# A clamp moved from VectorE to GpSimd, and a new order of all steps, in a gated-recurrence and MLP kernel

## The chip, the cores and the metric

The kernel runs on one core of a Trainium2 chip. A core has five engines with an instruction queue each: TensorE (PE; its weight loads are listed as PEld), VectorE (DVE), ScalarE (ACT), GpSimd (POOL) and SyncE (SP). Each works through its queue in order and waits on semaphores for the others. All transfers of this kernel are issued by SP. SBUF is the memory that the engines work in, PSUM the memory that matmuls write to, DRAM the large memory outside. The metric is the time of one execution on the device in microseconds (us), lower is better; of several runs the median counts.

## The reference

Two blocks follow each other. The first is a recurrence over 768 tokens for 4 batches and 8 heads with 48 channels. Its state is a complex 48x48 matrix per head, which is turned and damped by a gate at every token:

```python
mag = np.sqrt(a_re * a_re + a_im * a_im)
scale = np.minimum(mag, 0.999) / (mag + 1e-06)
a_re_n, a_im_n = (a_re * scale, a_im * scale)
for t in range(S):
    new_re = ar * S_re - ai * S_im
    new_im = ar * S_im + ai * S_re
    S_re, S_im = (new_re + k_t v_t^T, new_im)
    y[:, :, t] = q_t S_re
```

The second takes `y` as 3072 tokens of 384 features and applies an MLP with 2048 hidden features and a slope per feature below zero:

```python
h = x @ w_in
g = np.maximum(h, 0.0) + alpha * np.minimum(h, 0.0)
out = g @ w_out
```

The two weight matrices come as 64-bit floats, everything else as 32-bit.

## The kernel before

**Gates.** The recurrence is worked off in chunks of 128 tokens. Ahead of it, nine gate tasks turn `a_re` and `a_im` into magnitudes and phases: three for the first batch (chunk 0, chunks 1 and 2, chunks 3 to 5) and two for each other batch (three chunks each). A gate task loads its rows (L248), computes magnitude and unit phase on ScalarE and VectorE (L251 to L299), multiplies the magnitudes up a tree (L316) and sends them to DRAM as `decs` (L321), and multiplies the phases up in chains (L336, L338, helper `product`), with a carry from one task to the next. L394 to L407 make the phase of each block, and L422 and L425 apply it to all tokens. The result goes to DRAM as `phs` (L427). Small operations of these tasks run on VectorE for the first batch and on GpSimd for the others. There are two buffers for gate tasks, so a later one may load when an earlier one's `phs` has landed.

**Units.** One unit is one chunk of one batch: 24 units. It loads `q` and `k` as `KQ` (L575, L577), the phases as `PP` (L586) and the magnitudes as `T` (L593), both back from DRAM in another layout, and `v` as `V` and `VL`. VectorE multiplies `KQ` by `PP` (L648). Then come six levels of distance 1, 2, 4 to 32 tokens: TensorE makes scores in PSUM (L662), VectorE multiplies `KQ` by decays from `T` (L701), ScalarE copies `W` for the next level (L719), and the scores are masked on VectorE (L686) or ScalarE (L683). Then `k` is transposed (L736, L738), TensorE forms the chunk's `k v^T` (L747), VectorE brings the state `St` forward (L777, L780), and TensorE adds up `y` (L768, L793). At the first unit of a batch `St` is loaded (L706) and multiplied by the first `k` (L709). ScalarE copies `y` out (L807), and it goes to DRAM as `ysc` (L812).

**MLP.** The tokens of the units are taken in 14 groups of 128 or 256 tokens (1, 1, ten times 2, 1, 1 units). For each group and each of 16 blocks of 128 hidden features, three matmuls make `ps_h` (L841), ScalarE makes a negated ReLU (L848), VectorE completes the slope (L850), and a matmul adds into the output (L860). That makes 224 feature groups. `ps_h` has two buffers.

**Weights.** `w_in` and `w_out` come in 16 pieces (L487). Task `to_f32` turns a piece into 32-bit floats from its two 32-bit words: ScalarE takes the absolute value of the high word (L503), VectorE raises it to at least `F64_SMALL` (L511) and shifts it left by 3 bits (L513), ScalarE prepares the low word and the sign (L505, L507), and VectorE adds the two (L515). Two buffers `top` are used in turn.

**The order.** Nothing is scheduled at run time. Every piece of work is a Python generator that yields before each of its steps; the string `ORDER` has 4316 letters, and each letter lets one generator issue its next step. So the string sets the order of the instructions in every engine's queue, SP's included:

```python
def run(self, order):
    for c in order:
        next(self.tasks[self.LETTERS.index(c)], None)
```

`A` to `I` are the nine gate tasks, `J` loads of the units, `K` the spreading of `v` in DRAM, `L` loads of `v`, `M` the weight pieces, `N` and `O` the conversion of `w_in` and `w_out`, `P` to `Z` and `a` to `m` the 24 units, `n` the loads of `xT` for the MLP, and `o` the MLP. The string was found by a planner outside the kernel. The costs and dependences in the yields (`DVE(n // 2, ta)` and the like) were input of that planner; in the kernel they do nothing.

Of the kernel before, what the change touches and what calls it, by code (L numbers as in the profile page):

```python
# [14 lines left out]
ALU = mybir.AluOpType  # L15
# [11 lines left out]
F64_SMALL = 1.125 * 2.0 ** -15  # L27


ORDER = (  # L30
    "AAAAAAAAAAAAAAAAAAAABBJBAAMMMMKMAAAAAAANNBAAAAAAAAAAAAAAABNBMAAAJAAAAAAAAAAJJBANALBABAABANBBBOBABBAB"
    "AABAAAAKAOBNABKKMBBOBBOKBBBLLLAOABBLLLLLLABMLLBABANAAAAABOABABNAAABAKBAABNNOBBBNBBBONOMLBBBBOBOBBBBB"
    "BBNBBBBNNBOBBNBBNOOOBBBBOBCBJJPCBBBBBBOBMCCCOPBJBJCBMJNBPMBNNPPBBBJPKKKKKKKKBBBCBBCBOCKCBCBCCCCPCPCK"
    "BPCPPOPJJJLJCCPNJJPNPCDDCCCCPPCPOCONCQPCOPCQPPPQPPPQPCPPQCQOCJPJPPJPPMJJNPNNNCQCQQCCOOPPPPPCPOCPCNCP"
    "PPCPNCOPCPPCJMQQLPCCQQCDCOJPCCNNMLDCONCCCCCNCCNJKMCMnKKRCCCKORNCNCJCRLJJDCCCRCCCCQCOOOCCRRCCQCOCOOMO"
    "COOCRRooooNCNKKoCooNooOKCOCLKKMKoKKDCoooCCCCooQQQQKCooRQQCCQQNQQooQDooDDLLCNoooCDQQCQoQoooooRoooQDDQ"
    "DDRLLLLLLLLDDDoDoRQRDDDCQDQDQQQRDQRJQQQEEooooRDRoooRQNEJJJoQQNQQJJQDDLDDDDSDRDROoEoooooooESSRDSDooRo"
    "NoDERRoNRoDoSDREEooooSDLLLooEDooooRRoSLLLRDDDDRooORRDDSDDEQLLLLLLLRSRDRRNRRRRDSRDDDDODDooooDDDDEoNES"
    "oJooooOSSNJJEoJRJRRRSSTLLLLLLLLooSSoooOoJRRKDDJRoELSTnOTTToSKKoDDDoooooTLoSDDDDDDDDDoSSSSoRLToEooKoT"
    "oSoooooSSoSooooooooTETDEooSLoSSLLoETDDDEDDDooooooDSoooSSSSSSTSoSJTSoDEJJEJJEKJDoooLJLDoDLLEDEEoLoSSE"  # L40
    "SSSSSTSoooJoUoTEEEEooDDooToDooooEooooooooTnLDDooooDooooooooDEUTooooooJJLDDJooooDoooEoooooooooUTooToo"
    "oLLLLLooTDTETLooooooUTEooUoTTEoDUoooTEoEUTLooTKooEUEToJToToooUETTTTTTTETEEEETJEEEFJFETUoLoUUooooooUV"
    "TLUoFoToooTTLLUUooLoToUooVFVoUoUUUUoUUoooooFoJJUUVLLTULLLLLLoooVEEEUFUVooUUUEEEooTooEEEEEEEEEEEUUVUU"
    "UJUVUVEEFooVEooooJJJJJWVooEEEEEJUoUUUVooWUVJVoUVWKWJUoUVoEVEVWoVEEJoEEEoJWWWoJJJoVVVoWVooooVWEWVVnoL"
    "LLLLoVXLLLLooooLLLEEFLVFELEEEEFoEoVooooooVVoEoWEoVoooVoooVVVVVVVVWVEVLWWWooooooJoFFWVFWWEWXFooVVWWEV"
    "WooVLLJLJVooooooooooLLLLLVFWEWWFWWFoooooooWooooVWWoooWLLLLLWWWWWoFXXFXXWEWWoFoWFXXJFJJJJLYXFoooooooo"
    "XFXXoFFFFKJJWGoWWWXooooFooooYYWYXGWWWFoXFooYXFXoooooFoYXXXYFooYFFGFoooooooooXXooYXXooXYGooFXooFXFFXo"
    "oooXXGooXXFFFoFFLnooGoGJYoGLLLLLLLLLLLLXXXXXFFFXXFFFFXFFXJYJJJJZoGoooKooYoGooJoooooooooGGoYXZYYGYFFF"
    "FFFFFFGGJZFoZoFoooZoooGGooooXYYYYXXYZZZooYYLFLLLLLLooLLLFFoLoLLZooooXXYKKFFFFYYFFZYoooooGYYoFooFFFYF"
    "LoFGYGGGFooKoJJJKKFGGGGoYYYYYYYYYJXZooooKZoJJaKKKooLFFFooZZZLoJoZLLLooFGJLLLLXLLoLoKGFFFFoFFoooooooG"  # L50
    "GGYFYZaZaaZZooZZooooGaZZFLLFJFoooooooYYYYYYooaaFoaooooaoooJooJooZaZZZaooooZoooFZnZGGaooaoGooGGooZZZZ"
    "ZZZZaZZZGJJJHaaGJbbHooooooooooooooobGaGoZGZZaaaaaJLJJabGGHZoGZZZJJbooooooGGGooGooooaLooJboaabbHHboLL"
    "ooooaboaHbLaooaooooooHooLLLoLLooLaaLLoooGGooGGbaaGGaaGGaaooGoaJGoGGGGGGGGGGGHabbcLLHaHbGcbHHHHJJJboo"
    "ooooooooJJboooobLLGGocoobobJoooobcGGGcbbbboooHoHGbccbcKJJLLLLGoooooaocLdHaLooaobaGGbcLbLKLooGGLabbba"
    "ooooooobbGbbcHbGbbboocncoooHbGGGGGGGooocHHbodoooJJoLLoHLLoLLGGGLLLGLLHoooooLLoHooHoHoooooccKdooooooH"
    "HHHHGoooooHHooodoGLHcdoocccccobbbbbbHbdJdooGooooHoodHcHdoooooooocccddocoHHHodHHJcJJJoooJcoooccocIooo"
    "odHccccccoHccdIcoodeoHJoHoodooHHHHdodHddddHccccHJeLcLJcoooLJLLLeooooooooddooccLeLJoHHooHeHHHHHHHHedd"
    "dLIeoLooodooHHddooooLLdoLLoJJdeHHHdddddIIdddonoILJodoeoooooeLooILLfoooHHHHHHoeeooJooJIooKKoooooeHHfd"
    "dfIfodLeoeLKeKfoKKoeoodoLddIdLJJffLLLLLLeeofoeeIoofeooeooooIeooIofHHIJHHIdoIIeeooJoooHHHooeKHHoIIeoe"
    "ooeeeofHHoooeHHHHeeeeeIHLILLoooeIoeJeJJffooooooooooooKeoffgJffooooooIIoooooooooLLHHooIHHIIIfeeeeegoo"  # L60
    "ofoooeegooooooooLfffffooooooofgfggJooofLfJooLfooLLfLKHgLofLLgoofogJoffffffffIgffnooogogooJJJhIIIIooL"
    "oooIIhogoohJoooohIgLfJffLLgooooofffoIggoooooooooohLhLLLIgghgIggJLgLLgJooIooooggohgoIoIghofoooooohhgI"
    "IogoIIhgooohooooooLIIILIggggggggIJJhJooJhhgLLLhhiohoooooooIIoooohhhhhooooohohJooJgIIIIIIhhLLLIIIILhI"
    "IiooLooggooggihhhIoiooogoooooohIIIILIgJLLLLLoohoooooioIIooIIIIoIoohhohhhhhhihJoJnJiiiJJJJooooooooohI"
    "IIIIIIiooIjooIIoIIioiooIoooIIIooooojijiiooooooooLoojiooooIoojhLiILLiLLIoLoooiiiiJoLLooLooohLhooooIho"
    "ihhihjjooiooooiioiijjoooiiojiLLLioiiiioooJJJjjiiiioooLoooJjjioojjojJokooooooooojjikiiijjjJJkLoooijoo"
    "oookokkjjLkoooLookojkojkoojiijjnooookojoooooooookjLLLoLooLLLLLLjjjjjJJJkJJjJLoooooLLLLLoojjjoooooooo"
    "ooooolJJLoooollLjjjkjjojkkloooooooooooooooljjLkkkkklkLkllkJooooooooooolllkLklkJJLJLoooooolLkooookook"
    "kkooooooookkkkkkkkkJJoomooooooookkmkkkloollooooooJJokmooookknloooooooooommlmLoollmlLlloooooooloLoooo"
    "ooooooomoLllmmLLLooooooooolooooooooooollloooolloooomLoLoLLLLLllllllmlmmmoomoooooooooooooollmooooolll"  # L70
    "lllmomlmmmmmLooooooooLLoLLLoooLLLooLooooooooooooooooooooooooooooooooolnooooooomooooooooooooooooomooo"
    "ooooooooooooomoooomoomooooLooLLoomooooooooommooommmmmmmmmmmmmmmnoooooooooooooooooooooooooooooooooooo"
    "oooooooooooooooooooooooooooooooooooooooooooooooooooooooooooooooooooooooooooooooooooooooooooooooooooo"
    "oooooooooooooooo")

# [27 lines left out]
def kernel(  # L103
# [32 lines left out]
    nc = tc.nc  # L136
    B, HP, _, D, S = q.shape
    H = 2 * HP
# [60 lines left out]
    DVE = ACT = POOL = PE = DMA = step  # L199
# [290 lines left out]
    def to_f32(dst, *key):  # L490

        n = 2 * DM
        ta = yield ACT(n + 100, ("raw", *key), takes=(R["top"],))
        raw = raws.pop(key)
        lo, hi = raw[:, :, :, 0], raw[:, :, :, 1]
        slot = slots.pop(0)
        top = tops[slot].rearrange("p (r e) -> p r e", r=dst.shape[1])
        top_u = top.bitcast(U32)

        def halfwords(z, dtype=U16):  # L500
            return z.rearrange("p r e -> p (r e)").bitcast(dtype)

        nc.scalar.activation(top, hi.bitcast(F32), AF.Abs)  # L503
        tl = yield ACT(n + 200)
        nc.scalar.activation(dst, lo, AF.Identity, scale=2.0 ** -51, bias=bias_two)  # L505
        tl = yield ACT(n + 100)
        nc.scalar.activation(halfwords(dst, BF16)[:, 1::2].rearrange("p (r e) -> p r e", r=dst.shape[1]), hi.bitcast(F32), AF.Sign, bias=bias_plus)  # L507
        raw_done(*key, tl)

        yield DVE(n // 2, ta)  # L510
        nc.vector.tensor_scalar(out=top, in0=top, scalar1=F64_SMALL, scalar2=None, op0=ALU.max)  # L511
        yield DVE(n // 2)
        nc.vector.tensor_scalar(out=top_u, in0=top_u, scalar1=3, scalar2=None, op0=ALU.logical_shift_left)  # L513
        t = yield DVE(n, tl)
        nc.vector._custom_dve(ADD32_U16LIMBS, out=halfwords(dst), in0=halfwords(top), in1=halfwords(dst))  # L515
        slots.append(slot)
        return t
# [125 lines left out]
    def unit(u):  # L643
# [59 lines left out]
        if c == 0:  # L703
            k_ = yield DMA(144, *[("state", u - 2)] * (u > 1), takes=(R["St"],))
# [3 lines left out]
            k_ = yield DVE(H * D, k_, ("start", 0))  # L708
            nc.vector.tensor_tensor(out=St, in0=St, in1=start[:, b].unsqueeze(2).to_broadcast([D2, H, D]), op=ALU.mult)  # L709
            state[b] = (St, k_)  # L710
        k_ = r
        for h in LEVELS:
# [12 lines left out]
            k_ = yield DVE(2 * H * HC, e, *[("decays", u)] * (h == 1))  # L725
# [23 lines left out]
        ek = e  # L749
# [23 lines left out]
        for s in range(1 if last else 2):  # L773
            before, known = states[s]
            k_ = yield DVE(H * D, known, takes=(R["St"],))
            St = work.tile([D2, H, D], F32, tag="St", name="St", bufs=3)
            nc.vector.tensor_tensor(out=St, in0=before, in1=T[:, :, TL - 4 + s:TL - 3 + s].to_broadcast([D2, H, D]),  # L777
                                    op=ALU.mult)
            k_ = yield DVE(H * D, ek)
            nc.vector.tensor_tensor(out=St, in0=St, in1=kv[s][0:D2], op=ALU.add)  # L780
            R["lv" if s else "misc"].put(k_)
            states.append((St, k_))
# [170 lines left out]
```

## Time and profile before

| | us |
|---|---|
| median of 5 runs | 866.51 |
| lowest and highest of them | 862.18, 868.98 |
| the profiled execution | 871.17 |
| span of the profiled execution, first to last instruction | 869.5 |
| TensorE busy | 713.3 |
| VectorE busy | 650.3 |
| ScalarE busy | 428.0 |
| GpSimd busy | 164.4 |

"Busy" is the time in which an engine has at least one instruction under way. A row of a group gives the line in the kernel, the engine, the operation, what is written and read with its shape (partitions x elements), the count, the busy time, the mean duration in nanoseconds, and the idle time of the engine before these instructions with what ended it. A row of the table of waits gives who waited for whom, the total, the times and the longest. A row of the timeline gives start and duration in us. The granted clock is the share of TensorE's full clock that it was given; over the whole span it was 0.957.

### The profile page before, as it was taken

How to read it: one execution, taken by the hardware profiler on the slowest of the kernel's cores; microseconds unless marked ns; L12 is line 12 of the kernel's file. 1: busy time of each engine (PE TensorE's matmuls, PEld its weight loads, DVE VectorE, ACT ScalarE, POOL GpSimd, SP SyncE). 2: the span in 40 equal slices, each digit the busy share in tenths (PEclk: the TensorE clock that was granted, in tenths of full speed). 3: DMA queues.
4: the chain of work that ended last, by engine and by line, in shares of the span. 5: the costliest groups of instructions: out<-in, count | busy, mean ns of one | idle time of the engine just before them, and what ended most of it. 6: DMA issues, size and time to landing. Idle time of an engine off the chain costs nothing.

```text
span 869.5 us, 26876 instructions
## 1 busy us (share of the span) xinstructions
PE 713.3 (82%) x11488; PEld 532.8 (61%) x11488; DVE 650.3 (75%) x1012; ACT 428.0 (49%) x913; POOL 164.4 (19%) x277
## 2 busy tenths in 40 slices
PE   0001436778999999999899999998999999999998
PEld 0000324556776767776577777776776677777776
DVE  5999999897988988998679978977658555542212
ACT  7777586847355555643565456533334324223221
POOL 3000000076134001750344062110230000000000
PEclk9999858789999999999899999999999999999999
DMA  7699986876889596569866877667574565312010
GB/s 209 167 266 178 261 240 180 204 161 122 218 192 179 124 205 178 130 146 253 157 138 125 224 170 158 143 158 168 106 149 110 125 131 113 75 38 49 26 38 9
DMA packets 194559, 130.92 MB, mean 151 GB/s; under 512 B 74504, under 2 KB 186248, under 8 KB 194440
## 3 DMA queue, kind: packets, MB, share of 16 engines
q1 hardware_dynamic: 194440, 129.20, 64.5%
q8 instruction: 90, 1.47, 0.8%
q14 instruction: 29, 0.24, 0.1%
HBM read 100.82 MB, written 35.71 MB: 157 GB/s over the span
## 4 chain that ended last, share of the span: by engine, by line
PE 62%; DVE 15%; DMA 13%; issue 3%; SPq 3%; ACT 2%; POOL 2%; DVEq 0%; ACTq 0%
PE ps_h L841 25%; PE ps_o L860 24%; DMA T<-decs 5%; PE ps_lv L662 4%; DMA phs<-gate 3%; DVE KQ L701 3%; PE ps_y L768 3%; PE ps_y L793 2%; PE ps_kv L747 2%; DVE gate L336 2%; DVE gate L422 1%; POOL gate L336 1%; DMA PP<-phs 1%; PE ps_kt L736 1%; DVE gate L338 1%
## 5 line engine op out<-in xcount | busy, mean ns | idle before, releaser
L841 PE MATMUL ps_h<-xT,w_in_sb 128*128 128x256 f32 (+1 forms) x1344 | 313.5, 365 | 10.1 <-DVE g_sb L850 5.6
L860 PE MATMUL ps_o<-w_out_sb,g_sb 128*128 128x384 f32 x768 | 300.0, 505 | 10.3 <-DVE g_sb L850 6.2
L841 PEld LDWEIGHTS ps_h<-xT,w_in_sb 128*128 128x128 f32 x1344 | 238.6, 199 | 82.9 <-DVE g_sb L850 8.5
L701 DVE TENSOR_TENSOR KQ<-KQ,T 96x1024 f32<-96x1024 f32 x144 | 177.2, 1239 | 45.2 <-PE ps_lv L662 38.5
L848 ACT ACTIVATE g_sb<-ps_h 128x256 f32<-128x256 f32 (+1 forms) x224 | 79.0, 353 | 255.3 <-PE ps_h L841 254.5
L850 DVE SCALAR_TENSOR_TENSOR g_sb<-g_sb,al,ps_h 128x256 f32<-128x256 f32 (+1 forms) x224 | 97.2, 437 | 119.7 <-ACT g_sb L848 119.2
L860 PEld LDWEIGHTS ps_o<-w_out_sb,g_sb 128*128 128x128 f32 x768 | 139.9, 195 | 63.7 <-DVE g_sb L850 9.1
L662 PE MATMUL ps_lv<-KQ,W 96*32 96x32 f32 x3840 | 56.1, 205 | 50.6 <-ACT W L719 43.5
L719 ACT COPY W<-KQ 96x512 f32<-96x512 f32 x120 | 73.8, 622 | 42.7 <-DVE KQ L701 42.0
L662 PEld LDWEIGHTS ps_lv<-KQ,W 96*32 96x32 f32 x3840 | 44.4, 116 | 75.5 <-ACT W L719 50.1
L662 PE MATMUL ps_lv<-KQ 96*32 96x32 f32 x768 | 12.0, 205 | 72.3 <-DVE KQ L648 55.5
L648 DVE TENSOR_TENSOR KQ<-KQ,PP 96x2048 f32<-96x2048 f32 x24 | 56.5, 2354 | 16.6 <-DMA PP<-phs 14.8
L336 POOL TENSOR_TENSOR gate<-gate 128x72 f32<-128x72 f32 x42 | 29.0, 690 | 153.9 <-ACT gate L366 151.1
L662 PEld LDWEIGHTS ps_lv<-KQ 96*32 96x32 f32 x768 | 9.5, 117 | 75.9 <-DVE KQ L648 55.5
L683 ACT ACTIVATE A<-ps_lv,rows 128x64 f32<-128x64 f32 x144 | 40.3, 332 | 21.4 <-PE ps_lv L662 21.0
L336 DVE TENSOR_TENSOR gate<-gate 128x576 f32<-128x576 f32 (+5 forms) x84 | 47.5, 566 | 1.3
L768 PE MATMUL ps_y<-A,VL 64*48 64x64 f32 x2304 | 40.5, 222 | 3.9 <-DMA VL<-vsc 3.7
L422 DVE TENSOR_TENSOR gate<-gate 128x1152 f32<-128x1152 f32 (+2 forms) x36 | 43.2, 1214 | 0.1
L807 ACT COPY yT<-ps_y 48x256 f32<-48x256 f32 x96 | 31.3, 366 | 21.9 <-PE ps_y L793 21.2
L768 PEld LDWEIGHTS ps_y<-A,VL 64*48 64x48 f32 x2304 | 38.8, 124 | 4.2 <-DMA VL<-vsc 3.9
L686 DVE TENSOR_TENSOR A<-ps_lv,mask 128x256 f32<-128x256 f32 x96 | 39.5, 413 | 0.0
L780 DVE TENSOR_TENSOR St<-St,ps_kv 96x384 f32<-96x384 f32 x44 | 24.1, 548 | 15.5 <-PE ps_kv L747 12.5
(100 smaller groups left out, 760.6 us busy)
## 6 DMA issues: line engine op xcount, KB each, us to landing
T<-decs SPq DMA_DIRECT2D x48, 384.0 KB
PP<-phs SPq DMA_DIRECT2D x48, 193.5 KB
KQ<-in_q_dram SPq DMA_DIRECT2D x48, 192.0 KB
decs<-gate SPq DMA_DIRECT2D x7, 1152.0 KB
phs<-gate SPq DMA_DIRECT2D x14, 576.0 KB
KQ<-in_k_dram SPq DMA_DIRECT2D x40, 192.0 KB
vsc<-in_v_dram SPq DMA_DIRECT2D x48, 144.0 KB
VL<-vsc SPq DMA_DIRECT2D x24, 288.0 KB
```

The lines of the kernel that those rows point to most:

```text
L336: on(4 * k).tensor_tensor(out=m, in0=w[:, 1::-1].unsqueeze(2).to_broadcast([P, 2, 2, k]), in1=pairs_of(u), op=ALU.mult)
L422: TT(out=m[:, a], in0=U5[:, 1 + a], in1=turned(off3, o)[:, a].unsqueeze(1).unsqueeze(3).to_broadcast([P, L // 2, nb, 2]), op=ALU.mult)
L648: nc.vector.tensor_tensor(out=KQ, in0=KQ, in1=bass.AP(tensor=PP.tensor, offset=PP.offset, ap=[PP.ap[0], (1, 2), (P + 1, H), (1, P)]), op=A ...
L662: nc.tensor.matmul(t[64 * i + j:64 * i + j + HC // 2, p], lhsT=weights(4 * i + p)[:, j:j + HC // 2], rhs=q_[:, m * g:m * (g + 1)], start=T ...
L683: nc.scalar.activation(a[:, :, cols], t[:, :, at:at + name], AF.Copy, scale=s)
L701: nc.vector.tensor_tensor(out=x, in0=x, in1=m, op=ALU.mult)
L719: nc.scalar.copy(W.rearrange("p n t -> p (n t)").rearrange("p (m h) -> p m h", h=h), halves(KQ[:, 1].rearrange("p n t -> p (n t)"), h)[:, ...
L768: nc.tensor.matmul(o, lhsT=Vp[h][64 * i:64 * i + 64, s, e_ * D:(e_ + 1) * D], rhs=a, start=False, stop=False)
L841: nc.tensor.matmul(p, lhsT=w_in_sb[:, f // 2, kk, f % 2 * P:(f % 2 + 1) * P], rhs=x_of[m][:, kk], start=(kk == 0), stop=(kk == NK - 1))
L848: nc.scalar.activation(gt, p, AF.Relu, scale=-1.0)
L850: nc.vector.scalar_tensor_tensor(out=gt, in0=gt, scalar=al_1[:, f:f + 1], in1=p, op0=ALU.mult, op1=ALU.add)
L860: nc.tensor.matmul(sums[0], lhsT=gt[:, c * P:(c + 1) * P], rhs=w_out_sb[:, f], start=(f == 0), stop=(f == NF - 1))
```

## The change

The clamp L511 of the 16 weight pieces is issued to GpSimd instead of VectorE. The planner's cost of that step changes with it, and the second step of the state's update now names the first as something that it depends on, which the kernel itself ignores. With these costs, and with transfers that land late by a random time in the planner's model, the string `ORDER` was found anew. It has as many letters, and every generator as many steps, as before: VectorE has 16 instructions fewer, GpSimd 16 more, and TensorE, ScalarE and SP have the same instructions in another order.

```diff
 ORDER = (
-    "AAAAAAAAAAAAAAAAAAAABBJBAAMMMMKMAAAAAAANNBAAAAAAAAAAAAAAABNBMAAAJAAAAAAAAAAJJBANALBABAABANBBBOBABBAB"
-    "AABAAAAKAOBNABKKMBBOBBOKBBBLLLAOABBLLLLLLABMLLBABANAAAAABOABABNAAABAKBAABNNOBBBNBBBONOMLBBBBOBOBBBBB"
...
+    "AAAAAAAAAABBAMMABMAAAAAMNAAAMMAAAAAAAAABKAAAAAAJKBBNBAKJANAAAJONNAAAAAAOBNOAAAAAAAAAAAJAAAKKAAAAAAKK"
+    "KBABKLMAMKKKAAAAAAAAAAAAABBAAAAAAAAAALLLNLNOBBBBBBBBBBBBBBBOKKLJBBJBCOCNBBBBNNBBBNNNKNBBNNBBBBBOPBBO"
...
@@ to_f32
-        yield DVE(n // 2, ta)
-        nc.vector.tensor_scalar(out=top, in0=top, scalar1=F64_SMALL, scalar2=None, op0=ALU.max)
-        yield DVE(n // 2)
+        ta = yield POOL(1.4 * n, ta)
+        nc.gpsimd.tensor_scalar(out=top, in0=top, scalar1=F64_SMALL, scalar2=None, op0=ALU.max)
+        yield DVE(n // 2, ta)
         nc.vector.tensor_scalar(out=top_u, in0=top_u, scalar1=3, scalar2=None, op0=ALU.logical_shift_left)
@@ unit
-            k_ = yield DVE(H * D, ek)
+            k_ = yield DVE(H * D, ek, k_)
             nc.vector.tensor_tensor(out=St, in0=St, in1=kv[s][0:D2], op=ALU.add)
```

## The prediction

> **What bounds the kernel now.** The page's first two parts come first, because they say which engine is short and when. TensorE (PE) is busy 713.3 of 869.5 us, VectorE (DVE) 650.3; by slices VectorE is full in the first half, TensorE in the second, and GpSimd (POOL) is nearly empty from 30 to 150 us.
>
> ```profile
> PE 713.3 (82%) x11488; PEld 532.8 (61%) x11488; DVE 650.3 (75%) x1012; ACT 428.0 (49%) x913; POOL 164.4 (19%) x277
> PE   0001436778999999999899999998999999999998
> DVE  5999999897988988998679978977658555542212
> POOL 3000000076134001750344062110230000000000
> ```
>
> The table by stage sharpens this. Columns: stretch, its length, busy time of PE, PEld, DVE, ACT and POOL, granted clock, DMA share, GB/s.
>
> ```profile
> 60.00:120.00 60.00, 13.56 (x524) 11.59 (x524) 55.92 (x97) 40.15 (x55) 0.12 (x1) 0.86 0.99 239
> 120.00:220.00 100.00, 71.86 (x1358) 55.70 (x1359) 92.42 (x138) 65.56 (x128) 33.98 (x46) 0.81 0.72 167
> 220.00:310.00 90.00, 85.46 (x1507) 64.12 (x1507) 81.47 (x110) 46.41 (x112) 19.40 (x36) 0.98 0.79 174
> 480.00:840.00 360.00, 354.55 (x5230) 263.14 (x5229) 219.03 (x313) 134.15 (x343) 40.32 (x79) 0.99 0.52 118
> ```
>
> To 120 us VectorE and the transfers are both full, to about 310 us VectorE is (TensorE close behind), and from 480 us TensorE is. All 16 clamps lie between 22.9 and 185.8 us, where VectorE sets the pace.
>
> Next, VectorE's waits before 310 us (total, times, longest), then the two waits at unit 12, where the start of a batch costs most:
>
> ```profile
> DVE KQ L701 <- PE ps_lv L662: 5.3, 6, 1.5
> DVE KQ L648 <- DMA PP<-phs: 4.2, 3, 1.9
> DVE KQ L701 <- DMA T<-decs: 1.4, 2, 0.8
> ...
> 413.46 2.29 DVE L648 TENSOR_TENSOR KQ<-KQ,PP 96x2048 f32<-96x2048 f32 x1 [2.51 <-DMA PP<-phs]
> 419.15 0.55 DVE L709 TENSOR_TENSOR St<-St,start 96x384 f32<-96x384 f32 x1 [2.61 <-DMA St<-in_v_dram]
> 425.75 2.08 PE L841 MATMUL ps_h<-xT,w_in_sb 128*128 128x256 f32 x4 [4.07 <-DVE g_sb L850]
> ```
>
> Behind those two VectorE waits an L850 stands in the queue, and TensorE waits 4.07 us for it: a late transfer reaches TensorE through VectorE's order.
>
> Last, what GpSimd and VectorE do to each other (rows of minimum/median/maximum ns, then two pairs in time):
>
> ```profile
> L511 DVE TENSOR_SCALAR top<-top x16: 546/552/678, 22.9 to 185.8; 128x768 f32<-128x768 f32 x16
> L405 POOL TENSOR_SCALAR gate<-gate x6: 311/358/2232, 215.0 to 649.1; 128x144 f32<-128x144 f32 x6
> L403 POOL TENSOR_TENSOR gate<-gate x6: 487/754/2137, 213.9 to 648.5; 128x144 f32<-128x144 f32 x6
> L407 POOL TENSOR_TENSOR gate<-gate x6: 792/834/1778, 215.5 to 651.4; 128x288 f32<-128x288 f32 x6
> L385 POOL COPY carry<-run x3: 189/189/189, 202.6 to 518.8; 128x6 f32<-128x6 f32 x3
> ...
> 215.52 0.88 POOL L407 TENSOR_TENSOR gate<-gate 128x288 f32<-128x288 f32 x1
> 215.67 2.88 DVE L648 TENSOR_TENSOR KQ<-KQ,PP 96x2048 f32<-96x2048 f32 x1
> ...
> 182.32 4.23 POOL L336 TENSOR_TENSOR gate<-gate 128x72 f32<-128x72 f32 x1
> 188.89 2.28 DVE L648 TENSOR_TENSOR KQ<-KQ,PP 96x2048 f32<-96x2048 f32 x1
> ```
>
> L648 takes 2.28 us alone and 2.88 when a GpSimd instruction had started 0.15 us before it; a GpSimd L336 takes 4.23 us under a run of VectorE work. They stop each other.
>
> **The change part by part.** The sum goes along one path: VectorE up to feature group 54 (of 224, counted from 0; a group is three matmuls L841, one L848, one L850), then TensorE to the end. I add the mean durations by shape in each kernel's VectorE order up to the L850 of group 54, and TensorE's work after that group in TensorE's order, at the spacing that its matmuls had after 480 us (0.462 us for a 128x256 feature matmul, 0.677 for an output matmul; 690.4 us for all). Before: 308.6 and 546.6. The L850 of group 54 started at 309.0 in the trace, so the VectorE sum tracks time there (overlap of neighbours offsets 26.9 us of waits). 309.0 + 546.6 = 855.6; the last group started at 863.4 with 2.7 left, 866.1, so 10.5 us of stalls come after group 54, and 3.4 us of output end the span at 869.5.
>
> *The clamp leaves VectorE.* 16 x 0.560 us = 9.0 us by the row's mean. It is already out of the sum of the new order.
>
> *The clamp on GpSimd.* No row shows 128x768 there. Low end: L405, the same operation, is 311 ns at its shortest; a 128x6 copy is 189, leaving 0.85 ns per element, so 189 + 650 = 0.84 us. High end: L403 to L407 grow by 305 ns for 144 elements, 2.12 ns each, so 311 + 624 x 2.12 = 1.63 us. I take 0.84, the same operation. Its lateness is covered: in the new order 3.9 to 17.5 us of VectorE work stand between a clamp's place and its L513, but for the third clamp with none (at most one clamp). On GpSimd the last clamp has its place 14 us of VectorE work ahead of the chain L336/L338 of the fourth gate (160.3 and 174.4 in VectorE's sum), so the chain doesn't wait for it; memsets L303 and L247 stand between the clamps and cost 0.1 us each.
>
> *What it does to VectorE meanwhile.* For L394 (0.676 us alone) and L407 (0.792), the longest GpSimd instructions now, the VectorE instruction behind them lost 0.20 and 0.32 us on average over all 18 (0 to 0.60), some 35%. So 16 x 0.84 x 0.35 = 4.7 us. Ends: 0, if GpSimd always finds a gap, and 16 x 1.63 = 26.1, if VectorE stands still for all of it.
>
> The Trainium skill, "SBUF — State Buffer", section "Who interferes with whom", speaks against this part: the pair of ports that VectorE and GpSimd share is an exclusive lock, and an instruction of VectorE with two SBUF inputs and a GpSimd one that reads SBUF exclude each other, whoever is second waiting for the whole of the first. The 2.88 against 2.28 us agrees in kind; the average over 18 does not, since the second is often GpSimd. By the rule taken at its worst the sum would carry 13.4 us in place of 4.7.
>
> *The order, up to group 54.* VectorE's sum is 311.7 there, against 308.6: 3.1 more although the clamps are gone, so 12.1 us of other work has been put ahead. TensorE has 542.4 us left in place of 546.6. The transfers stand alike: before the second unit's PP, 16.2 MB are ahead on SP in both orders; before its T 17.5 against 16.8; before the first xT 25.4 against 25.8. The waits on VectorE before 310 us I leave at 26.9: longer distances for transfers, shorter ones on the chip (the rivals price both).
>
> *The order, after group 54.* Between the step that writes the last phs of a gate (L427) and the L648 that needs it (5.7 us for the write and 5.6 for the read at 308 us in the chain of waits), TensorE's work grows at unit 12 from 3.4 to 13.8 us and at unit 18 from 5.1 to 7.9, and falls at unit 9 from 9.5 to 7.7. That takes away 2.5 (the wait shown) and 2.8 (TensorE's one wait for L648, near 590 us) and adds 1.8. The distance from the St load (L706) to L709 falls to nothing at all four batches, from 0.4 to 3.2 us; the wait shown, 2.61, stays. Stalls: 10.5 - 2.5 - 2.8 + 1.8 = 7.0. Ends: 0, and 17 with three more such waits.
>
> Sum: 309.0 + 3.1 + 4.7 + 542.4 + 7.0 + 3.4 = 869.6 against 869.5. The profiled execution took 871.17 us, 1.67 around its span, and the median of five runs, 866.51, is 0.9947 of that: 871.3 x 0.9947 = 866.6 us. No change, that is within 0.5% (862.2 to 870.8), which is about what a measurement of this kernel can tell.
>
> **The rivals.**
>
> *Faster: 856 us.* GpSimd works in VectorE's gaps, p = 0, and the longer distances (unit 3: 6.8 to 13.6 us of TensorE work, unit 6: 11.0 to 19.6) remove the 4.2 + 1.4 us of transfer waits before 310: 869.6 - 4.7 - 5.6 = 859.3, or 856.4 as a median. For it: from group 66 to the end of VectorE's load the two sums together are some 14 us lower than before (group 84: 844.0 against 857.6), so a stall there has less to push. Against: the port, and the bound at group 54 (854.1 against 855.2) hardly moves.
>
> *Slower by the port: 875 us.* Every clamp stops VectorE for its 0.84 us: 13.4 in place of 4.7, 878.3, or 875.3. For it: VectorE is 93% busy from 60 to 120 us, and seven instructions behind an L394 or L407 lost 0.39 to 0.60 us. Against: in the trace GpSimd more often waits. It decides above 0.56 us per clamp; the high end, 1.63, gives 888.
>
> *Slower by VectorE waiting for scores: 877 us.* In the first twelve units, 40 of the 72 level steps L701 have under 1 us of VectorE work between their score matmuls and themselves in the new order, 28 in the old. At 0.88 us (5.3 over 6), twelve more cost 10.6 us: 880.2, or 877.1. It decides from five on. Against: most of the 28 cost nothing now.
>
> **How the numbers follow.** No change 0.33, faster 0.30, slower by the port 0.21, by the scores 0.16: so 0.30, 0.33, 0.37. The likeliest gives 866.6, its own range 862 to 871. Between 853 (faster case with 3 us of stalls less) and 884 (between the slower cases and the port's high end) lie 8 in 10.
>
> **What would show it.** Clamp rows on GpSimd near 0.84 us at their shortest, and VectorE's L701, L648 and two-input gate rows longer by 0.3 us where one runs. The L850 of group 54 near 317 us (309 + 3.1 + 4.7). At unit 12 no wait of L648 for PP; TensorE's busy time unchanged at 713. I am wrong if group 54 comes before 312 or after 322 us, or if TensorE's stalls after it are over 12 us.

## The result, and the profile after

The changed kernel takes 861.6 us (median; 858.4 to 864.9), the kernel before 864.2 in the same comparison. The ratio is 0.9971, with a 95% interval of 0.9960 to 0.9981: about 2.5 us faster, a gain that is small but not nothing. The forecast was 866.6 us and no change within 0.5%.

The profiled execution of before (span 869.5 us) was a longer one than usual. A second profile of the same kernel, e8 below, spans 862.2 us, and it is the one to set beside the 860.5 us of after. The page of after, the same four lines as shown of before:

```profile
PE 706.4 (82%) x11488; PEld 532.0 (62%) x11488; DVE 655.3 (76%) x996; ACT 426.9 (50%) x913; POOL 190.7 (22%) x293
PE   0000324876998999999999999999999999999998
DVE  5999989999976999789978987798767665444212
POOL 5212322449303200440034005300052000000000
```

TensorE's digits come later (from the fourth slice 0, 3, 2, 4 where before had 1, 4, 3, 6) and then hardly leave 9. VectorE's busy time rose from 650.3 to 655.3 us although it lost 16 instructions. The table by stage of after, with the columns of the one before (length, busy time of PE, PEld, DVE, ACT, POOL, granted clock, DMA share, GB/s):

```profile
60.00:120.00 60.00, 13.84 (x492) 11.81 (x492) 57.63 (x88) 40.89 (x58) 15.33 (x7) 0.93 0.83 199
120.00:220.00 100.00, 62.87 (x1357) 48.83 (x1360) 97.56 (x138) 68.55 (x124) 52.21 (x50) 0.73 0.80 190
220.00:310.00 90.00, 83.84 (x1531) 64.19 (x1529) 73.62 (x103) 42.22 (x110) 19.08 (x37) 0.94 0.74 162
480.00:840.00 360.00, 358.40 (x5288) 267.33 (x5288) 228.03 (x326) 139.80 (x351) 41.85 (x82) 1.00 0.54 120
```

From 120 to 220 us VectorE is busier than before (97.56 against 92.42) and TensorE idler (62.87 against 71.86), and TensorE runs more of it at half clock (0.73 against 0.81). From 480 us TensorE is busy for 358.40 of 360 us, 354.55 before. So the new order starts the MLP later and then runs it more smoothly. The L850 of feature group 54 divides the two parts:

| kernel | group 54 at | from there to the end | VectorE busy / idle up to there | TensorE busy / idle after |
|---|---|---|---|---|
| before, profile of the prediction | 309.0 | 560.5 | 278.1 / 30.9 | 542.8 / 17.7 |
| before, profile e8 | 309.6 | 552.6 | 278.0 / 31.6 | 537.7 / 14.9 |
| after | 328.6 | 531.9 | 293.7 / 34.9 | 526.6 / 5.4 |

Each idle time of TensorE has some 3.5 us at the very end in it, in which the last output goes out.

Against e8 the start loses 19.0 us and the rest wins 20.7. The net gain is the small difference of two larger moves. Part of both is only where group 54 stands among the other steps: at group 60 after is 8.6 us late (345.5 against 336.9 in e8), and from there to the end it wins 10.3. The waits of TensorE between 300 and 850 us (total, times, longest) in before, then in after:

```profile
PE ps_h L841 <- DVE g_sb L850: 5.6, 2, 4.1
PE ps_lv L662 <- issue: 3.6, 3, 1.9
PE ps_o L860 <- DVE KQ L648: 2.8, 1, 2.8
PE ps_h L841 <- DMA xT<-ysc: 0.9, 2, 0.6
```

```profile
PE ps_lv L662 <- issue: 1.6, 1, 1.6
PE ps_kt L736 <- DVE KQ L701: 0.2, 1, 0.2
```

In after, TensorE no longer waits for VectorE's L850 or L648 there. At unit 12, where before had L648 waiting 2.51 us and L709 2.61 us, the timeline of after shows both without a wait (a wait would stand in brackets at the end):

```profile
421.67 2.28 DVE L648 TENSOR_TENSOR KQ<-KQ,PP 96x2048 f32<-96x2048 f32 x1
427.64 0.55 DVE L709 TENSOR_TENSOR St<-St,start 96x384 f32<-96x384 f32 x1
```

A stall costs more than its length. In before, two stretches at half clock of 3.4 us each come with the wait of 4.07 us that ended at 425.75 (they begin at 423.8, still in the wait), and one comes behind the 2.75 us near 590 us. The table by stage of before, granted clock third from the end:

```profile
424.30:427.50 3.20, 1.75 (x4) 1.18 (x4) 1.78 (x4) 3.16 (x8) 1.52 (x6) 0.50 0.53 136
427.70:430.50 2.80, 2.80 (x69) 2.20 (x69) 1.95 (x2) 1.67 (x4) 2.41 (x6) 0.50 0.68 141
590.90:594.30 3.40, 3.32 (x7) 2.36 (x8) 2.91 (x5) 0.99 (x2) 0.00 (x0) 0.52 0.11 40
594.50:597.50 3.00, 3.00 (x72) 2.06 (x71) 0.48 (x1) 0.38 (x1) 0.00 (x0) 1.00 0.93 174
```

In after the clock is full without a break from 275.5 to 859.2 us.

The clamps are on GpSimd and do not look as forecast. The row of L511 in after, and three places of its timeline:

```profile
L511 POOL TENSOR_SCALAR top<-top x16: 2124/2452/7013, 13.1 to 168.5; 128x768 f32<-128x768 f32 x16
```

```profile
47.19 2.31 POOL L511 TENSOR_SCALAR top<-top 128x768 f32<-128x768 f32 x1 [2.66 <-ACT top L503]
47.42 0.98 DVE L338 TENSOR_TENSOR gate<-gate 128x192 f32<-128x192 f32 x1
48.44 0.56 DVE L336 TENSOR_TENSOR gate<-gate 128x384 f32<-128x384 f32 x1
49.03 0.36 DVE L338 TENSOR_TENSOR gate<-gate 128x192 f32<-128x192 f32 x1
...
131.79 2.34 POOL L511 TENSOR_SCALAR top<-top 128x768 f32<-128x768 f32 x1 [6.69 <-ACT top L503]
132.07 1.84 DVE L701 TENSOR_TENSOR KQ<-KQ,T 96x1024 f32<-96x1024 f32 x1
...
146.59 7.01 POOL L511 TENSOR_SCALAR top<-top 128x768 f32<-128x768 f32 x1 [12.45 <-DMA phs<-gate]
147.54 0.41 DVE L686 TENSOR_TENSOR A<-ps_lv,mask 128x256 f32<-128x256 f32 x1
147.87 1.34 DVE L277 TENSOR_TENSOR gate<-gate 128x1152 f32<-128x1152 f32 x1
149.13 1.35 DVE L296 SCALAR_TENSOR_TENSOR gate<-gate 128x1152 f32<-128x1152 f32 x1
150.40 1.22 DVE L701 TENSOR_TENSOR KQ<-KQ,T 96x1024 f32<-96x1024 f32 x1
...
151.87 1.64 DVE L296 SCALAR_TENSOR_TENSOR gate<-gate 128x1152 f32<-128x1152 f32 x1
```

A clamp takes 2.12 us at its shortest, but it stops VectorE for much less. The L338 behind it at 47.42 takes 0.98 us in place of 0.36, the L701 at 132.07 1.84 in place of 1.22; the second and third VectorE instructions run at full speed under the same clamp. At 146.59 it is the clamp that is held up, under a row of VectorE work, to 7.01 us; of that row only the second L296 is longer, by 0.3 us. Under each of the 16 clamps one VectorE instruction takes longer than the same shape does in e2 below, where GpSimd has no clamps: by 0.3 to 0.64 us, 8.9 us in all. (The 8.2 us that the expectation of e1 names is too low; the L316 of 128x384, for one, takes 1.06 us under a clamp and 0.56 in e2, and occurs only once in each kernel.)

### The profile page after: what moved, and what is told of

Its sections match the earlier page's. It is cut to its first block, busy times and chain, and to the rows that moved or that the text cites. A ratio compares the mean times of both kernels' runs of the same rounds, so it can differ in the third digit from the quotient of the medians.

```text
span 860.5 us, 26855 instructions
## 1 busy us (share of the span) xinstructions
PE 706.4 (82%) x11488; PEld 532.0 (62%) x11488; DVE 655.3 (76%) x996; ACT 426.9 (50%) x913; POOL 190.7 (22%) x293
## 3 DMA queue, kind: packets, MB, share of 16 engines
q8 instruction: 90, 1.47, 0.8%
## 4 chain that ended last, share of the span: by engine, by line
PE 75%; DVE 13%; issue 3%; ACT 3%; DMA 3%; SPq 2%; DVEq 0%; ACTq 0%
PE ps_o L860 29%; PE ps_h L841 28%; PE ps_lv L662 5%; PE ps_y L768 4%; PE ps_kv L747 3%; PE ps_y L793 3%; DVE KQ L701 2%; PE ps_kt L736 2%; DVE gate L336 2%; DVE gate L338 1%; SPq L625 1%; DMA V<-in_v_dram 1%; DVE gate L316 1%; DMA KQ<-in_q_dram 1%; DVE gate L296 1%
## 5 line engine op out<-in xcount | busy, mean ns | idle before, releaser
L841 PE MATMUL ps_h<-xT,w_in_sb 128*128 128x256 f32 (+1 forms) x1344 | 304.1, 358 | 0.0
L841 PEld LDWEIGHTS ps_h<-xT,w_in_sb 128*128 128x128 f32 x1344 | 234.4, 194 | 69.9 <-issue 1.8
L701 DVE TENSOR_TENSOR KQ<-KQ,T 96x1024 f32<-96x1024 f32 x144 | 177.5, 1243 | 46.5 <-PE ps_lv L662 43.0
L850 DVE SCALAR_TENSOR_TENSOR g_sb<-g_sb,al,ps_h 128x256 f32<-128x256 f32 (+1 forms) x224 | 97.5, 437 | 127.4 <-ACT g_sb L848 126.8
L860 PEld LDWEIGHTS ps_o<-w_out_sb,g_sb 128*128 128x128 f32 x768 | 137.9, 192 | 57.2 <-DVE g_sb L850 9.0
L511 POOL TENSOR_SCALAR top<-top 128x768 f32<-128x768 f32 x16 | 43.6, 2724 | 85.8 <-ACT top L503 73.0
L648 DVE TENSOR_TENSOR KQ<-KQ,PP 96x2048 f32<-96x2048 f32 x24 | 55.3, 2302 | 0.0
L768 PE MATMUL ps_y<-A,VL 64*48 64x64 f32 x2304 | 43.7, 227 | 11.7 <-issue 9.2
L336 DVE TENSOR_TENSOR gate<-gate 128x576 f32<-128x576 f32 (+5 forms) x84 | 48.3, 575 | 3.2 <-ACT gate L308 1.4
L683 ACT ACTIVATE A<-ps_lv,rows 128x64 f32<-128x64 f32 x144 | 39.1, 331 | 20.7 <-PE ps_lv L662 20.3
L768 PEld LDWEIGHTS ps_y<-A,VL 64*48 64x48 f32 x2304 | 40.9, 128 | 13.5 <-issue 10.9
L336 POOL TENSOR_TENSOR gate<-gate 128x72 f32<-128x72 f32 x42 | 20.0, 475 | 128.9 <-ACT gate L366 126.0
L686 DVE TENSOR_TENSOR A<-ps_lv,mask 128x256 f32<-128x256 f32 x96 | 39.5, 413 | 0.0
```

Source lines behind the costliest of these rows:

```text
L336: on(4 * k).tensor_tensor(out=m, in0=w[:, 1::-1].unsqueeze(2).to_broadcast([P, 2, 2, k]), in1=pairs_of(u), op=ALU.mult)
L511: nc.gpsimd.tensor_scalar(out=top, in0=top, scalar1=F64_SMALL, scalar2=None, op0=ALU.max)
L648: nc.vector.tensor_tensor(out=KQ, in0=KQ, in1=bass.AP(tensor=PP.tensor, offset=PP.offset, ap=[PP.ap[0], (1, 2), (P + 1, H), (1, P)]), op=A ...
L701: nc.vector.tensor_tensor(out=x, in0=x, in1=m, op=ALU.mult)
L768: nc.tensor.matmul(o, lhsT=Vp[h][64 * i:64 * i + 64, s, e_ * D:(e_ + 1) * D], rhs=a, start=False, stop=False)
L841: nc.tensor.matmul(p, lhsT=w_in_sb[:, f // 2, kk, f % 2 * P:(f % 2 + 1) * P], rhs=x_of[m][:, kk], start=(kk == 0), stop=(kk == NK - 1))
```

## The experiments

Two theories stood at first. **Wash and order:** the clamp's move saves VectorE about as much as the port costs it, and the new order carries what gain there is, by a later start and a rest without stalls. **The clamp helps:** the move itself carries the gain and the order only rearranges.

### e1 and e2: one part of the change at a time

e1 is before with the new `to_f32`, e2 is after with the old one:

```diff
 e1 (ORDER of before), e2 the other way round (ORDER of after)
-        yield DVE(n // 2, ta)
-        nc.vector.tensor_scalar(out=top, in0=top, scalar1=F64_SMALL, scalar2=None, op0=ALU.max)
-        yield DVE(n // 2)
+        ta = yield POOL(1.4 * n, ta)
+        nc.gpsimd.tensor_scalar(out=top, in0=top, scalar1=F64_SMALL, scalar2=None, op0=ALU.max)
+        yield DVE(n // 2, ta)
```

> The order of before, with the clamp L511 on GpSimd at the same places. Theory (the clamp is a wash: VectorE gets 16 x 0.56 = 9.0 us back and loses the 8.2 us by which instructions behind a clamp were longer in the changed kernel): ratio 0.998 to 1.005, above 1 where L513 comes up before its clamp is done, since that order left 0.8 to 6.2 us of VectorE work between them and a clamp takes 2.1 us or more. Rival (the clamp is the gain, the order nothing): ratio 0.990 to 0.995.

> The new order, with the clamp on VectorE at its place in that order. Theory: the order carries the whole difference, ratio 0.995 to 0.999; the L850 of group 54 at 326 to 331 us as in the changed kernel (328.6), TensorE idle under 7 us after it. Rival (the clamp is the gain): ratio 1.003 to 1.008, group 54 near 337 us.

The clamp alone gave 1.0025 (1.0000 to 1.0051), the order alone 0.9979 (0.9956 to 1.0003). With the clamp alone group 54 came at 309.9 us, after 309.6 in e8, and the rest took 554.9. With the order alone it came at 326.4 and the rest took 533.6, nearly all that after shows. So the order moves both parts, and the clamp's move is a wash by itself, if anything a small loss. The interval of e2 just includes no change: that the order gains as a whole rests on the two parts in the profiles and on after's own ratio, not on e2's time alone. In e1 the clamps are as long as in after:

```profile
L511 POOL TENSOR_SCALAR top<-top x16: 2125/2182/4592, 15.6 to 192.9; 128x768 f32<-128x768 f32 x16
```

### e3 and e4: no clamp at all

Both leave the clamp of the weights out, e3 from before and e4 from after; what is left is each order without its 16 clamps.

```diff
 e4 (e3 the same with ORDER of before)
         ta = yield POOL(1.4 * n, ta)
-        nc.gpsimd.tensor_scalar(out=top, in0=top, scalar1=F64_SMALL, scalar2=None, op0=ALU.max)
         yield DVE(n // 2, ta)
```

> The order of before; the 16 clamps are left out, so small weights are not raised to the limit. It measures what the clamp costs as long as VectorE does it. Theory: VectorE is 7 to 9 us shorter up to group 54, of which 4 to 8 us reach the end: ratio 0.991 to 0.995. Rival (VectorE before group 54 doesn't set the end): ratio 0.998 to 1.001.

> The new order; the 16 clamps are left out, so small weights are not raised to the limit. It measures what the clamp costs on GpSimd. Theory (port): group 54 comes 6 to 9 us earlier than in the changed kernel (320 to 323 us) and the end as much, ratio to before 0.987 to 0.992. Rival (a clamp on GpSimd is free): the same time as the changed kernel, ratio 0.996 to 0.998.

e3 gave 0.9948 (0.9919 to 0.9976), e4 0.9925 (0.9898 to 0.9952), both against before. The 16 clamps thus cost 0.5% on VectorE, and 0.9971 - 0.9925, again about 0.5%, on GpSimd. The engine that does it makes no difference that these intervals can tell. The rival of e4, a free clamp, falls; its ratio and group 54 both lie just outside the theory's bands (0.992 and 323). e3's profile is of its longest execution (864.5 us, median 855.2), so its marks are rough. Group 54 came at 305.9 in e3 and 323.4 in e4: without any clamp on either side the new order is 17.5 us later there, as it is with clamps on VectorE on both sides (326.4 against 309.0: 17.4).

### e5 and e6: the old front with the new rest

If the late start and the smooth rest were two separate effects, before's order up to some point and after's behind it would have both an early start and a smooth rest, some 2% faster than either. `ORDER` is before's letters up to feature group 54 (e5) or 24 (e6), then what is left of after's letters in their sequence; the clamps are on GpSimd.

```diff
 ORDER = (
-    after's 4316 letters
+    before's first 1544 letters (e5; 1028 in e6), then after's letters without those
...
```

> The clamp on GpSimd; the order of before up to the L850 of feature group 54, and from there the steps that are left in the sequence of the new order. Theory (two separate effects: a later start, 309 to 329 us, and a rest without stalls, 560 to 532 us, that add up): group 54 near 310 us, the rest 532 to 548 us, ratio 0.980 to 0.993. Rival (the late start pays for the smooth rest: the work that the new order does early has to be done): group 54 near 310 us, the rest 550 us or more, ratio 0.997 to 1.005.

> The clamp on GpSimd; the order of before up to the L850 of feature group 24, then the new order's sequence of what is left. Theory (two separate effects): group 24 near 220 us in place of 228.5 of the changed kernel, and the end up to 8 us earlier, ratio 0.988 to 0.995. Rival (start pays for the rest): ratio 0.996 to 1.002, group 54 as late as in the changed kernel.

e5 gave 1.0006 (0.9987 to 1.0025), e6 0.9985 (0.9964 to 1.0006). The theory of two separate effects fell: neither gained what it forecast.

The marks need care, since the old front ends just ahead of the L850 that names it: its last groups are 53 in e5 and 23 in e6. In e5 group 53 still came at 308.0 us, as in before (308.6), and group 54 at 324.0, 16.0 us later, where before has 0.4 us between the two. In these 16 us TensorE is busy for 8.6 us, at a granted clock of 0.73. It is the work that after's order has ahead of its next MLP steps: it had to be issued first. Counted from group 53, e5's rest takes 549.0 us, 553.0 in e8 and 534.5 in after, so of the 18.5 us only 4.0 are won, less than the 7.9 by which two profiles of before differ; the smooth 533.0 us behind group 54 start after the catching up. In e6 the same step lies between group 23 (220.0) and group 24 (229.9); group 54, far behind it, came at 326.2, near after's 328.6, and the rest took 531.7. The gain of the old front was gone. The late start pays for the smooth rest.

### e7: stalls put back on purpose

To price a stall, 36 extra VectorE instructions of 0.96 us each (34.5 us) were put ahead of L850 in after's order, six at a time, in six token groups of the MLP. They change no value.

```diff
         r = yield DVE(n + 45, r, first=True)
+        if f == 8 and 5 <= m <= 10:
+            for _ in range(6):
+                nc.vector.tensor_tensor(out=tops[1], in0=tops[1], in1=tops[1], op=ALU.max)
         nc.vector.scalar_tensor_tensor(out=gt, in0=gt, scalar=al_1[:, f:f + 1], in1=p,
```

> The changed kernel with six instructions of 128x768 (about 0.95 us each) on VectorE ahead of one L850 in each of six MLP groups between 430 and 730 us; they change nothing that is used. Theory (a stall costs TensorE twice, the idle time and a stretch at half clock behind it): six half-clock stretches appear behind six TensorE waits of 2 to 5 us, and the time grows by the idle time plus about half of the half-clock time. Rival (a stall costs its idle time alone): granted clock stays 1.00 from 480 to 840 us, and the time grows by the idle time.

The ratio is 1.0335 (1.0286 to 1.0383). From group 80 to group 176 it took 361.2 us against 333.2 in after, 28.0 more. TensorE's idle time grew by 18.7 us (20.3 against 1.6), and its busy time, for the same matmuls, by 9.3 us (340.9 against 331.6), with 17.1 us at half clock where after has none. The half clock came at four of the six places, twice as long at one of them. Half of 17.1 is 8.6, so the clock covers nearly all of the 9.3. By this a microsecond of stall costs 28.0 / 18.7 = 1.5 us. One of the stretches, and the waits behind them:

```profile
572.90:579.50 6.60, 5.13 (x10) 3.50 (x11) 6.57 (x10) 1.00 (x2) 0.00 (x0) 0.50 0.31 85
```

```profile
PE ps_h L841 <- DVE g_sb L853: 10.7, 5, 4.0
PE ps_y L793 <- DVE St L780: 5.8, 2, 3.0
```

Of 34.5 us of extra VectorE work about 18.7 us reached TensorE as a wait; the slack of the new order took the other half.

### e8: before once more

No edit, a second profile of before, because the first was a longer execution.

> The kernel before, for another profiled execution. Theory: the structure repeats (group 54 at 305 to 311 us, TensorE idle over 12 us after it, with half-clock stretches behind the waits at units 9, 12 and 18), span 858 to 870. Rival (the profile of before was an odd one): under 5 us idle after group 54 and no half-clock stretch.

It took 863.9 us with a span of 862.2. Its stalls of TensorE at unit 12 and near 587 us are there again. The lines of unit 12, and the wait near 587:

```profile
411.38 2.29 DVE L648 TENSOR_TENSOR KQ<-KQ,PP 96x2048 f32<-96x2048 f32 x1 [1.96 <-DMA PP<-phs]
417.12 0.56 DVE L709 TENSOR_TENSOR St<-St,start 96x384 f32<-96x384 f32 x1 [2.67 <-DMA St<-in_v_dram]
423.71 1.66 PE L841 MATMUL ps_h<-xT,w_in_sb 128*128 128x256 f32 x4 [3.89 <-DVE g_sb L850]
```

```profile
PE ps_o L860 <- DVE gate L336: 3.2, 1, 3.2
```

Near 587 us L648 itself waited for no transfer this time, so a late PP isn't needed for the second stall. Half-clock stretches follow at 424.2 to 427.6 and 588.0 to 591.4 us. The half-clock stretches of the first profile at 328 and 690 us are not in it, and of the three places that the theory named the one at unit 9 is missing. e1 and e3, which keep before's order, have one near 327 us again, but none at 690.

### e9: the new front with the old rest

The mirror of e5: after's letters up to feature group 54, then what is left of before's in their sequence. It asks whether the smooth rest is bought by work that the new front puts ahead, or by how the new rest is arranged.

```diff
 ORDER = (
-    after's 4316 letters
+    after's letters up to the L850 of group 54, then before's letters without those
...
```

> The new order's front up to feature group 54, then before's sequence of what is left; clamp on GpSimd. If the smooth rest is bought by work that the new front puts ahead (slack): group 54 at 324 to 330 us, the rest 530 to 545 us with TensorE idle under 8 us after group 54, ratio 0.995 to 1.005. If the smooth rest comes from how far the new sequence keeps the transfers and level steps from their users after group 54: group 54 at 324 to 330 us but the rest 548 to 555 us, TensorE idle over 10 us with two or more stretches at half clock, ratio 1.01 to 1.02.

The ratio is 1.0017 (0.9999 to 1.0035). Group 54 came at 329.8 us, the rest took 535.4, with no stretch at half clock after group 54 (0.4 us in all). TensorE was idle for 8.3 us after it, just over the 8 that the first theory gave. Its waits between 300 and 850 us (line numbers are one higher in this kernel):

```profile
PE ps_lv L663 <- issue: 1.4, 2, 0.7
PE ps_h L842 <- DVE g_sb L851: 1.4, 1, 1.4
PE ps_h L842 <- issue: 1.3, 1, 1.3
PE ps_h L842 <- DMA xT<-ysc: 1.1, 1, 1.1
```

With the old rest behind the new front 17 of the 20.7 us are kept: it is mostly the work put ahead that makes the rest smooth. The arrangement of the rest adds about 3.5 us between single profiles (535.4 against 531.9). The ratios say the same more firmly: 1.0017 here and 0.9971 for after, intervals apart, 0.46% or some 4 us. So neither the new front with the old rest (e9) nor the old front with the new rest (e5) gains; the margin of 2.5 us needs the new rest behind the new front. (In the series of e9 and e10 before took 865.7 us, in those of e1 to e8 860.6 and 860.8, so times in us compare only roughly between them, and the ratios decide.)

### e10: each clamp done twice

```diff
         ta = yield POOL(1.4 * n, ta)
         nc.gpsimd.tensor_scalar(out=top, in0=top, scalar1=F64_SMALL, scalar2=None, op0=ALU.max)
+        nc.gpsimd.tensor_scalar(out=top, in0=top, scalar1=F64_SMALL, scalar2=None, op0=ALU.max)
         yield DVE(n // 2, ta)
```

> The kernel after with each of the 16 clamps done twice on GpSimd. If a clamp takes the port from VectorE for some 0.5 to 0.63 us whatever its own length, VectorE's busy time up to feature group 54 rises by 6 to 10 us over the kernel after (293.7 us) and the ratio is 1.000 to 1.008. If VectorE is held up only by the first of two back to back, or the new order has slack for it, busy rises by under 3 us and the ratio stays at 0.996 to 0.999.

The ratio is 1.0080 (1.0059 to 1.0101), at the top of the first theory's band, and the busy time a little above it. VectorE's busy time up to group 54 rose from 293.7 to 303.9 us: 10.2 us for 16 more clamps, 0.64 each. A pair in the timeline (L512 is the second clamp), then the row of L512:

```profile
43.72 2.47 POOL L511 TENSOR_SCALAR top<-top 128x768 f32<-128x768 f32 x1 [0.83 <-ACT top L503]
44.18 0.86 DVE L338 TENSOR_TENSOR gate<-gate 128x192 f32<-128x192 f32 x1
...
46.27 2.12 POOL L512 TENSOR_SCALAR top<-top 128x768 f32<-128x768 f32 x1
46.41 1.10 DVE L336 TENSOR_TENSOR gate<-gate 128x384 f32<-128x384 f32 x1
```

```profile
L512 POOL TENSOR_SCALAR top<-top x16: 2123/2495/4217, 15.4 to 180.6; 128x768 f32<-128x768 f32 x16
```

Each clamp of the pair stops one VectorE instruction, by 0.50 and 0.54 us here (0.36 and 0.56 alone). Group 54 came 12.3 us later than in after, and the span grew by 12.4: the rest (532.0 us) gave nothing back. By the ratios, 1.0080 against 0.9971, the second clamps cost 1.1%, some 9.4 us or 0.59 each. Here a delay of the start was paid in full at the end; the rest had no stalls left to absorb it.

The starts and rests of the eleven profiles without extra work in the rest (e7 is left out) fall into two clusters. Where group 54 came at 306 to 310 us the rest took 553 to 561; where it came at 323 to 341 the rest took 530 to 535. (e5 is in the second cluster because the mark lies behind its catching up.)

## Why the prediction was right and wrong

**The bound.** Right as far as it was tested: e10 adds VectorE time in the first 185 us and it arrives in full at group 54 and at the end (12.3 and 12.4 us); e7 adds stalls after group 54 and they arrive too. From 220 to 310 us, though, the prediction's own row has TensorE busier than VectorE (85.46 against 81.47 of 90 us), not close behind it; which of the two sets the time there was not tested.

**The clamp on GpSimd.** The length was wrong, 2.12 us against a range of 0.84 to 1.63. The step that failed is the scaling of L405 by 0.85 ns per element, from a pair of small rows of different operations; between L405 (311 ns, 144 elements) and the clamp (2124 ns, 768 elements) it is 1813 / 624 = 2.9. The share of 35% failed the other way, since clamps of 2.1 to 7.0 us stop VectorE for at most 0.64 us in after. Together the port term came out at 8.9 us (the sum over the 16 clamps) against 4.7 forecast. The rival "slower by the port" set its point of decision at 0.56 us per clamp; the mean was 8.9 / 16 = 0.56, right on it, and by e1 the move was a wash. The sum gave the move a gain of 4.3 us (9.0 less 4.7); with 8.9 it is 0.1, nothing.

The Trainium skill, "SBUF — State Buffer", section "Who interferes with whom", was weighed at that step. It calls the shared pair an exclusive lock, and says of VectorE's two-port modes that whoever issues first holds it for the whole instruction; the prediction took that for two-input instructions too. The direction was right and the trace disagrees on the length: one VectorE instruction under a clamp of 2.1 to 3.0 us lost 0.38 to 0.64 us and the ones after it nothing.

**The order up to group 54.** Forecast 12.1 us of work put ahead, and with the clamp 317; measured 328.6. By e2 the order alone is worth 17.4 (15.2 us of VectorE's busy time and 2.2 of waits). So 5.3 us of the miss are the order's, and the remaining 6.5 are the clamp: -4.3 forecast, +2.2 measured from e2 to after (0.4 us of VectorE's busy time and 1.8 of its waits, between single profiles). The prediction's own test, "wrong if group 54 comes after 322 us", went against it. Why VectorE was busy for 15.2 us rather than 12.1 was not traced further.

**The waits before 310 us left as they were.** Nearly right as a sum and wrong in its parts. The waits of L648 for PP and of L701 for T are gone, as the rival "faster" had it; the waits for scores grew, as the rival "slower by VectorE waiting for scores" had it, though by 3.8 us and not 10.6. L850's wait for ScalarE, which the prediction's lines leave out, grew as well, by 2.8 us. In before, then in after, up to 310 us:

```profile
DVE g_sb L850 <- ACT g_sb L848: 5.1, 5, 3.2
```

```profile
DVE KQ L701 <- PE ps_lv L662: 9.1, 6, 3.7
DVE g_sb L850 <- ACT g_sb L848: 7.9, 5, 4.5
```

VectorE's idle time up to group 54 went from 30.9 to 34.9 us.

**TensorE's rest.** This is the step that failed most: 542.4 + 7.0 + 3.4 = 552.8 forecast, 531.9 measured. The prediction priced TensorE's work after group 54 at the mean spacing after 480 us (0.462 us for a feature matmul and 0.677 for an output matmul) and took all of that for work that no order can change. But the mean has idle time and half clock in it: from 480 to 840 us TensorE of before was idle for 5.4 us (354.55 of 360 busy) and ran at half clock for 6.8 us, at 591.0 and 690.0. Only the 10.5 us that the sum left over counted as stalls. The medians of the same spacings in the same trace are 0.432 and 0.645; with 411 feature matmuls of this size and 326 output matmuls behind group 54, that is some 22 us less in either order. In after the means fell to 0.451 and 0.664, the medians stayed at 0.432 and 0.645: the matmuls did not become faster, what lay between them became less.

Against the profile that the prediction started from, TensorE's busy time after group 54 fell by 16.2 us (542.8 to 526.6) where 4.2 were forecast, and its idle time by 12.3 (17.7 to 5.4) where 3.5 were forecast. Of the 12.0 us of busy time beyond the forecast some 7.9 are the clock (17.1 to 1.4 us at half clock, halved); the other 4.1 are left without a cause that was shown. Part of the miss is that this profile was a long one: in e8 the rest of before is 7.9 us shorter.

**The stalls.** Right in kind, too small in size. The two waits at units 12 and 18 went, as forecast from the longer distance between L427 and L648. The wait for St at L709 was forecast to stay and went as well; and the clock behind a stall was not in the sum as a term. Of the 20.7 us that the rest won against e8, 9.5 are idle time of TensorE, some 3.3 the clock (7.9 to 1.4 us at half speed, halved) and 4.2 the work put ahead (the prediction's 546.6 to 542.4); 3.7 are left without a cause that was shown.

**The sum.** The errors offset each other: 11.8 us too early at group 54 and 20.9 too long after it give a span 9.1 too long, 869.6 against 860.5. The time of 861.6 us lies just below the 862.2 to 870.8 that the prediction called no change, and below its own range from 862, inside the wide one from 853 to 884. That the total came so close is luck: it is the small difference of two large moves, of which the prediction saw only a part.

## What to carry to other kernels

Take idle time and slow-clock stretches out of the spacing by which an engine's remaining work is priced, and add them as terms of their own: a mean spacing has them inside, and a change that removes stalls then looks worth too little. Medians for the two main kinds of matmul come near here, worked out afterwards: 542.4 less 22, plus 5.4 of idle time and 0.7 for the clock, is some 526 us, against 531.9 measured. When an operation moves between VectorE and GpSimd, the price is how long it stops the other engine, not how long it takes; here 0.56 us saved and 0.56 us paid (0.64 for the second clamps of e10) made a wash. An order that does work ahead against late transfers buys a rest without stalls with a later start; compare the two at a fixed mark in the middle, because the total alone hides both.

## What the runs showed of the hardware that was not expected

- A clamp of 128x768 floats takes 2.12 us on GpSimd at its shortest and 0.55 us on VectorE, but in after it stops VectorE only once and for at most 0.64 us. Of the 32 clamps of e10 one stopped VectorE twice (L336 and L514, 0.63 us each, under the clamp at 99.08), and the longest stop was 0.68 us. Not every VectorE instruction is stopped: L850 and L686, which take one input from PSUM, ran at 0.34 and 0.41 us under clamps of after (168.66 and 147.54). GpSimd can be held up for longer in turn: 7.01 us for the same instruction under a row of VectorE work.
- A gap of 1.9 to 4.1 us in TensorE's work is mostly followed by one or two stretches of 3.4 us at half clock: at 283.8, 423.8 (two), 591.0 and 690.0 us in before, 424.2 and 588.0 in e8, 572.8 (two), 634.3 and 695.7 in e7. It is not certain: gaps of 2.91 us in e7 at 513 us and of 1.94 in e5 at 287 us had none. Shorter gaps mostly have none (1.65 us at 325 and 1.82 at 389 in e8, 1.54 at 391 in before), but the half clock at 328.2 in before followed 1.26 us, the one at 606.3 in e2 1.58, and the one at 453.4 in e7 two gaps of 1.08 and 1.47. So the length alone does not decide, and no threshold is shown.
- The Trainium skill, "TensorE: Matmul & The Clock Gate", section "HAM oscillation — how this bites in real kernels", gives as the rule that TensorE must have no idle gaps above about 3.4 us. The runs agree on the unit of 3.4 us but not on the threshold: gaps of 1.26, 1.89 and 2.75 us in before were followed by half clock.
